# Expert layers with routing woven in: a planner that counts VectorE work by spacing, and ScalarE's copies kept to the first half of a group of matmuls

## The chip, the cores and the metric

The kernel runs on one core of one Trainium2 chip, as one launch. The metric is device time in microseconds (us); three runs of the kernel before gave 767.39, 765.89 and 762.88, so its median is 765.89.

## The reference

Attention with a local window and 32 global tokens gives x, 4352 rows of 512. A gate then gives every row to one of 8 experts of exactly 544 places, greedily by the sorted logits, and each expert applies two layers to its rows:

```python
cap = N // E                              # 4352 // 8 = 544
logits = x @ w_gate
for idx in np.argsort(-logits.flatten()):
    tok, e = (int(idx) // E, int(idx) % E)
    if assigned[tok] >= 0 or counts[e] >= cap:
        continue
    assigned[tok] = e; counts[e] += 1
for e in range(E):
    mask = assigned == e
    out[mask] = np.maximum(x[mask] @ w1[e], 0.0) @ w2[e]
```

w1[e] is 512 x 1024, w2[e] is 1024 x 512, all float32.

## The kernel before, in words

Up to about 230 us of the profile the kernel does the attention (function `attention`), which the change leaves alone. Then a routing phase (`Routing.phase`, L556) finds one expert that fills up next and the 544 rows it gets, and from 277 us on the eight experts run one after another in `ffn` (L873), called groups 0 to 7 here. While TensorE (PE) multiplies for one expert, the routing phase for a later one is woven between its matmuls.

**One group.** First H = relu(x w1): 8 blocks f of 128 hidden columns by 2 halves of the expert's 544 rows; each of these 16 small groups is 12 matmuls of 128x272 (L893), which sum three products of high and low parts (x high by w1 high, x low by w1 high, x high by w1 low). After each, ScalarE (ACT) writes relu of it as `hh`, the high part (L895; for every second one also 32 columns into `h32`, L897), and VectorE (DVE) writes the rest as `hl` (L899, "H's low part"). An H tile lies in one of 4 PSUM buffers, which are free again when `hl` is made. Then small matmuls in plain float32 for the last 32 rows (L908), then four tiles Y = H w2 of 24 matmuls of 128x512 each (L918), each copied out by ACT (L866) and scattered by a DMA of GpSimd's queue (POOL).

**What has to be ready for the next group.** Its weights: `w1r` and `w2r` are gathered by POOL's queue (1 MB each, two of each per expert, L705); ACT copies a slice of 128x512 as the high part (`w1h`, `w2h`, L717), and DVE subtracts for the low part (`w1l`, `w2l`). Of the eight w1 slices, four hold columns that the first four blocks f read, four (tag "b") those of the last four blocks; what of the latter is not made by f = 4 is made there at once (`force(f"b{ph}")`, L885). Its rows: five gathers `xg` by the routing's result `idx`, then 20 transposes on PE into an H tile (L746), `xh` by ACT and `xl` by DVE.

**Routing.** A phase has a search of 8 steps (`search`, L516). A step is 18 small matmuls on PE (`r_G` by `r_oh`, the last of them `rem` by `one`), `r_ce` on DVE, 2 matmuls with `big`, a scan `r_pm` and a compare `r_G` on DVE, and so on: each engine waits for the other. After it come some 30 small DVE instructions, 34 matmuls with `rhs`, and `idx`.

**What sets the order.** Every engine runs its instructions in the order in which the Python program writes them, and waits at an instruction until its input is there. That order comes from a model of time in the program. `V.now` is PE's time: `step(ns)` (L806) adds 125 for an H matmul and 232 for a Y matmul, then writes out whatever has come due: `hl` (list `fill`), the low parts of slices (list `lag`), items of `todo` (gathers, copies, transposes, with a time and a condition each), and the next piece of routing. `V.busy` is DVE's time (`Queue`, L386): each instruction issued through it adds an estimated duration. Routing yields the time at which its next PE piece may be written: `ready()` (L393) is `V.busy` plus HOP. The copies of weight slices wait for `calm()` (L774): DVE less than 200 ns ahead and fewer than two subtractions outstanding. A group's end (L921) waits until everything for the next group has been written.

Of the kernel before, what the change touches and what calls it, by code (L numbers as in the profile page):

```python
# [369 lines left out]
TX = 22000  # L370
TW = 34000
AHEAD = 200
HOP = 400
SLACK = 100
PACE = 250
RELU = 700
# [9 lines left out]
class Queue:  # L386


    def __init__(s, eng):
        s.eng = eng  # L390
        s.now = s.busy = 0.0

    def ready(s):  # L393
        return s.busy + HOP
# [4 lines left out]
    def __getattr__(s, name):  # L399
        op = getattr(s.eng, name)  # L400

        def issue(*args, **kw):
            aps = [x for x in list(args) + list(kw.values()) if hasattr(x, "dtype") and hasattr(x, "shape")]
            n = max(int(np.prod(x.shape[1:])) for x in aps)
            fast = name in ("tensor_scalar", "tensor_copy") or name == "tensor_tensor" and all(
                mybir.dt.size(x.dtype) == 2 for x in aps)
            s.busy = max(s.busy, s.now) + 180 + n * (1.9 if "scan" in name else 0.5 if fast else 1.05)
            return op(*args, **kw)  # L408
        return issue


class Routing:
# [58 lines left out]
    def begin_ps(s, ctx):  # L471
        s.ps = ctx.enter_context(s.tc.tile_pool(name="rps", bufs=1, space=PSUM))

    def mm(s, out, *args, ns=60, **kw):
        s.nc.tensor.matmul(out, *args, **kw)  # L475
        s.V.now += ns
        s.V.busy = max(s.V.busy, s.V.now + 200)

    def t(s, name, shape, dt=F32):
        return s.sb.tile([128] + shape, dt, name="r_" + name)  # L480
# [35 lines left out]
    def search(s):  # L516
        nc = s.nc
        for it in range(NIT):
            yield -1
            yield s.when  # L520
            A = s.ps.tile([128, 2, E], F32, name="R")
            for i in range(18):
                j, r = slice(2 * i, 2 * i + 2), 32 * (i % 4)
                g, o = (s.G[:, j].rearrange("p a b -> p (a b)"), s.oh[:, j]) if i < 17 else (s.one, s.rem)
                s.mm(A[r:r + 32], g, o, ns=22, start=(i < 4), stop=(i >= 14))
            p = s.ps.tile([128, 16, E], F32, name="R2")
            if it == 0:
                lo = s.t("lo", [34], I32)
                lof = s.t("lof", [34])
                s.V.tensor_scalar(lo, s.u, 0xffff, None, op0=ALU.bitwise_and)  # L530
                s.V.tensor_scalar(lof, lo, 2.0 ** -16, None, op0=ALU.mult)
                s.x = s.hi
            else:
                x = s.t("x%d" % (it % 2), [34])
                if it == 3:
                    s.V.scalar_tensor_tensor(x, s.x, P, lof, op0=ALU.subtract, op1=ALU.add)
                else:
                    s.V.tensor_scalar(x, s.x, P, None, op0=ALU.subtract)
                s.x = x
            ce = s.t("ce", [2, 16, E], F16)  # L540
            s.V.tensor_tensor(ce, A[:, :, None, :].to_broadcast([128, 2, 16, E]),
                              s.dk[:, :, :, None].to_broadcast([128, 2, 16, E]), op=ALU.mult)
            when = s.V.ready()
            yield -1
            yield when
            for k in range(2):
                s.mm(p, s.big, ce[:, k], start=(k == 0), stop=(k == 1))
            pm = s.t("pm%d" % (it % 2), [16 * E])
            s.V.tensor_tensor_scan(pm, p.rearrange("p a b -> p (a b)"), s.fin[:, it], 0.0, op0=ALU.max,
                                         op1=ALU.min)  # L550
            P = pm[:, 16 * E - 1:16 * E]
            if it < NIT - 1:
                s.cand(s.x, P, it + 1)
        s.P = P.bitcast(I32)

    def phase(s, ph):  # L556
# [16 lines left out]
        a = s.t("a", [34])  # L573
# [18 lines left out]
        p = s.ps.tile([128, 68], F32, name="R")  # L592
# [4 lines left out]
        if more:  # L597
            g = s.t("gt", [34], BF16)
# [23 lines left out]
        rhs = s.rhs  # L622
# [3 lines left out]
        ohl = s.t("ohl", [64, 34], BF16)  # L626
        for k in range(4):
            q = slice(16 * k, 16 * k + 16)
# [10 lines left out]
        p = s.ps.tile([128, 64], F32, name="R2")  # L639
        for j in range(34):  # L640
            r = 32 * (j % 4)
            s.mm(p[r:r + 32], rhs[:, :, :, j].rearrange("p a b -> p (a b)"), ohl[:, :, j], ns=22, start=(j < 4),
                 stop=(j >= 30))
        if not last:
            s.V.scalar_tensor_tensor(s.act, s.wt, vs, s.act, op0=ALU.not_equal, op1=ALU.mult)
# [13 lines left out]
        p = s.ps.tile([128, 6], F32, name="R2")  # L659
# [26 lines left out]
def experts(ctx, tc, A, xd, ident, rt, out):  # L686
# [55 lines left out]
    def trans_x(xg, t, late):  # L742
        n = sizes[t]
        p = ps.tile([128, 4, 128], F32, name="H", bufs=4)
        for d in range(4):
            nc.tensor.transpose(p[:, d, :n], xg[t][:n, 128 * d:128 * d + 128], ident[:n, :n])  # L746
        q = slice(128 * t, 128 * t + n)
        split(xh[:, :, q], xl[:, :, q], p[:, :, :n], late, SPLIT + 4 * 110)
# [12 lines left out]
    V = rt.V  # L761
    V.now = V.busy = 0.0
    pool, dma, need = [0.0], [0.0], [0.0]
    fill, lag, todo, raw1 = [], [], [], {}
    done, cur, mid, wrote = [False], [0], [-1], [0.0]

    def pool_op(ns, nbytes=0):
# [4 lines left out]
        return pool[0]  # L772

    def calm():  # L774
        return V.busy < V.now + AHEAD and len(lag) < 2

    def chain():
        for ph in range(1, E):
# [10 lines left out]
    def at(tag, t, f, cond=None):  # L789
        todo.append((tag, t, cond, f))  # L790

    def pending(*tags):
        return any(x[0] in tags for x in todo)
# [12 lines left out]
    def step(ns):  # L806
        V.now += ns
        low()
        settle()
        for i, (tag, t, cond, f) in enumerate(todo):  # L810
            if t <= V.now and (cond is None or cond()):
                todo.pop(i)
                f()
                break
        while not done[0] and V.now >= need[0]:
            v = next(routing, None)
            if v is None:
                done[0] = True
            elif v >= 0:
                need[0] = v  # L820
# [21 lines left out]
    def get_x(p):  # L842
        xg = load_x(p)
        for t in range(5):
            r = pool_op(1040, sizes[t] * 2048)
            at(f"x{p}", r, lambda t=t: trans_x(xg, t, True), lambda: mid[0] == p - 1)

    def get_w2(p):
        def go(k):
# [23 lines left out]
    def ffn(ph):  # L873
        nxt = ph + 1
        t0 = V.now
        cur[0] = ph
        half = []
        if nxt < E:
            at(f"g{nxt}", t0, lambda: get_w1(nxt, half), lambda: nxt in rt.widx and not pending(f"b{ph}"))
            at(f"h{nxt}", t0, lambda: get_x(nxt), lambda: nxt in rt.idx and (mid[0] == ph or V.now > t0 + TX))  # L880
            at(f"v{nxt}", t0, lambda: get_w2(nxt), lambda: mid[0] == ph and nxt in rt.widx and
               (not pending(f"h{nxt}") or V.now > t0 + TW))
        for f in range(8):
            if f == 4:
                force(f"b{ph}")  # L885
                half.append(True)
            for hf in range(2):
                q = slice(HF * hf, HF * hf + HF)
                p = ps.tile([128, HF], F32, name="H", bufs=4)
                fs = slice(128 * f, 128 * f + 128)  # L890
                for d in range(4):
                    for k, (w, x) in enumerate(((w1h, xh), (w1h, xl), (w1l, xh))):
                        nc.tensor.matmul(p, w[d][:, fs], x[:, d, q], start=(d + k == 0), stop=(d + k == 5))  # L893
                        step(125)
                nc.scalar.activation(hh[:, f, q], p, AF.Relu)  # L895
                if hf:
                    nc.scalar.activation(h32[:, f], p[:, HF - 32:HF], AF.Relu)  # L897
                low(len(fill) > 1)
                fill.append((V.now + RELU, lambda p=p, f=f, q=q: V.scalar_tensor_tensor(  # L899
                    hl[:, f, q], p, 0.0, hh[:, f, q], op0=ALU.max, op1=ALU.subtract)))  # L900

        low(True)
        force(f"w{ph}")

        p = ps.tile([128, 128], F32, name="Y", bufs=2)
        for f in range(8):
            for c in range(4):
                nc.tensor.matmul(p[32 * c:32 * c + 32], h32[:, f], w2r[f // 4][:, f % 4, 128 * c:128 * c + 128],  # L908
                                 start=(f == 0), stop=(f == 7))
            step(220)  # L910
        mid[0] = ph
        out_tile(ph, 4, p)
        for t in range(4):
            p = ps.tile([128, DM], F32, name="Y", bufs=2)
            for f in range(8):
                q = slice(128 * t, 128 * t + 128)
                for k, (h, w) in enumerate(((hh, w2h), (hh, w2l), (hl, w2h))):
                    nc.tensor.matmul(p, h[:, f, q], w[f], start=(f + k == 0), stop=(f + k == 9))  # L918
                    step(232)
            out_tile(ph, t, p)  # L920
        while nxt < E and (pending(f"g{nxt}", f"h{nxt}", f"a{nxt}", f"x{nxt}", f"v{nxt}") or nxt not in raw1):  # L921
            step(120)
        settle(True)

# [7 lines left out]
    xg = load_x(0)  # L932
# [96 lines left out]
```

## Time and profile before

| | us |
|---|---|
| median of three runs | 765.89 |
| the profiled execution, its own time | 761.97 |
| its span, first to last instruction | 760.2 |
| PE busy | 698.3 |
| DVE busy | 506.1 |
| ACT busy | 305.6 |
| POOL busy | 159.6 |
| groups 0 to 7, from the first H matmul to the last Y matmul | 470.66 |

Names in rows read "written tile <- read tiles"; L12 is line 12 of the kernel. A row of the windows view gives the stretch (us from the span's start), its length, the busy time of PE with the number of instructions, the TensorE clock that was granted (1.00 is full), the share of the DMA engines and GB/s. In a row of the timeline the first two numbers are start and duration, and brackets hold the idle time before and what ended it. A matmul's busy time overlaps the next one's, so the lengths of stretches count, not sums of busy time.

### The profile page before, as it was taken

The page shows a single profiled execution, that of the slowest core. Times are in us where ns is not written, and L with a number is a line of the kernel's source. Part 1 is how long each engine was busy: PE and PEld are TensorE (multiplying, and loading weights), DVE is VectorE, ACT ScalarE, POOL GpSimd, SP SyncE. Part 2 cuts the span into 40 slices and gives each one's busy share as a digit, 9 for nine tenths or more (in the row PEclk, how much of TensorE's full clock was granted, in tenths as well). Part 3 has the DMA queues.
Part 4 walks back from the last instruction along what each step waited for, and adds up shares of the span by engine and source line. Part 5 has one row for each costly group of instructions (what it writes and reads, how often), then busy time and mean ns, then how long its engine had stood idle before and what let it go on. Part 6 is the DMA issues. An engine that isn't in the chain of part 4 may idle for free. (4 is left out here: it accounts for less than half of the span.)

```text
span 760.2 us, 21827 instructions
## 1 busy us (share of the span) xinstructions
PE 698.3 (92%) x9012; PEld 571.8 (75%) x9012; DVE 506.1 (67%) x1855; ACT 305.6 (40%) x841; POOL 159.6 (21%) x190
## 2 busy tenths in 40 slices
PE   7899999999995289989999998999998999999993
PEld 6667777777773179778878877877876987988982
DVE  5787787778686777666776766766766766651400
ACT  4656766656650034233323323414322333552310
POOL 5222221121100130340150043034034015231011
PEclk9999999999997569999999999999999999999998
DMA  8998879869601160260080062054036008251000
GB/s 347 409 364 325 321 276 334 323 239 337 253 20 57 64 217 1 94 233 15 6 304 32 6 252 86 1 176 165 1 106 235 1 12 312 104 199 55 2 32 28
DMA packets 32418, 120.55 MB, mean 159 GB/s; under 512 B 6720, under 2 KB 6976, under 8 KB 24128
## 3 DMA queue, kind: packets, MB, share of 16 engines
q1 hardware_dynamic: 22080, 67.78, 23.9%
q0 software_dynamic: 10240, 51.39, 19.0%
q8 instruction: 71, 1.16, 0.6%
q14 instruction: 27, 0.22, 0.1%
HBM read 101.32 MB, written 17.83 MB: 157 GB/s over the span
## 5 line engine op out<-in xcount | busy, mean ns | idle before, releaser
L893 PE MATMUL H<-xh,w1h 128*128 128x272 f32 x512 | 154.3, 301 | 1.9 <-ACT w1h L717 1.9
L893 PE MATMUL H<-xl,w1h 128*128 128x272 f32 x512 | 153.9, 301 | 2.2 <-DVE xl L408 2.2
L893 PE MATMUL H<-xh,w1l 128*128 128x272 f32 x512 | 151.8, 296 | 1.0 <-DVE w1l L408 1.0
L145 ACT ACTIVATE p<-p,nm 128x128 f32<-128x128 f32 x256 | 81.8, 392 | 67.9 <-DVE ls L165 35.5
L895 ACT ACTIVATE hh<-H 128x272 fp32r<-128x272 f32 x128 | 50.9, 397 | 137.9 <-PE H L893 131.4
L918 PE MATMUL Y<-w2l,hh 128*128 128x512 f32 x256 | 103.2, 403 | 0.0
L918 PE MATMUL Y<-w2h,hh 128*128 128x512 f32 x256 | 103.0, 402 | 0.0
L918 PE MATMUL Y<-w2h,hl 128*128 128x512 f32 x256 | 102.1, 399 | 0.0
L893 PEld LDWEIGHTS H<-xh,w1h 128*128 128x128 f32 x512 | 99.1, 194 | 4.0 <-ACT w1h L717 3.0
L893 PEld LDWEIGHTS H<-xl,w1h 128*128 128x128 f32 x512 | 99.1, 194 | 3.8 <-DVE xl L408 3.2
L893 PEld LDWEIGHTS H<-xh,w1l 128*128 128x128 f32 x512 | 99.0, 193 | 2.2 <-DVE w1l L408 2.1
L408 DVE SCALAR_TENSOR_TENSOR hl<-H,hh 128x272 fp32r<-128x272 f32 x128 | 55.7, 436 | 31.3 <-ACT h L897 20.5
L717 ACT ACTIVATE w1h<-w1r 128x512 fp32r<-128x512 f32 x64 | 37.7, 626 | 94.8 <-DMA w1r<-in_w_dram,widx 58.8
L134 PE MATMUL S<-qk,qz 128*64 128x128 f32 x1024 | 70.5, 279 | 5.7 <-DVE qz L86 3.0
L86 POOL COPY qz<-q 64x544 f32<-64x544 f32 x60 | 38.2, 636 | 149.0 <-DMA q<-in_qk_dram 133.1
L134 PEld LDWEIGHTS S<-qk,qz 128*64 128x64 f32 x1024 | 54.9, 136 | 18.4 <-issue 14.2
L141 DVE CUSTOM_DVE_ANT_0 p<-S,mask 128x128 f32<-128x128 f32 x256 | 58.6, 285 | 6.9 <-DMA mask<-in_mask_dram 2.8
L918 PEld LDWEIGHTS Y<-w2h,hh 128*128 128x128 f32 x256 | 48.1, 188 | 12.7 <-issue 2.8
L918 PEld LDWEIGHTS Y<-w2l,hh 128*128 128x128 f32 x256 | 48.2, 188 | 9.7
L918 PEld LDWEIGHTS Y<-w2h,hl 128*128 128x128 f32 x256 | 48.2, 188 | 9.7
L408 DVE TENSOR_TENSOR w1l<-w1r,w1h 128x512 fp32r<-128x512 f32 x64 | 42.9, 687 | 18.4 <-ACT w1h L717 18.2
L408 DVE TENSOR_TENSOR w2l<-w2r,w2h 128x512 fp32r<-128x512 f32 x64 | 41.9, 685 | 16.2 <-ACT w2h L717 15.4
(165 smaller groups left out, 1130.7 us busy)
## 6 DMA issues: line engine op xcount, KB each, us to landing
vw<-in_vw_dram SPq DMA_DIRECT2D x32, 1040.0 KB, 7.8
qk<-in_qk_dram SPq DMA_DIRECT2D x32, 432.0 KB, 5.4
q<-in_qk_dram SPq DMA_DIRECT2D x32, 272.0 KB, 6.0
xd<-xs SPq DMA_DIRECT2D x8, 1024.0 KB, 6.3
xd<-xg SPq DMA_DIRECT2D x64, 8.0 KB, 5.6
xg<-xd,idx POOLq DMA_INDIRECT x40, 3.7
mask<-in_mask_dram SPq DMA_DIRECT2D x1, 512.0 KB, 6.1
cf<-in_cf_dram SPq DMA_DIRECT2D x1, 512.0 KB, 12.4
```

What stands on the lines that cost most here:

```text
L86: eng.tensor_copy(z[r, :, h, :], q[r].rearrange("p (j i) -> p j i", i=32))
L134: nc.tensor.matmul(st[64 * r:64 * r + 64, c, :], z[:, j].rearrange("p h i -> p (h i)"), kw[:, k0:k0 + 128], start=True, stop=True)
L141: nc.vector.tensor_tensor_reduce(s.p[:, c, :], st[:, c, :], mask[:, 4 * s.u + c, :], 1.0, -BIG, ALU.add, ALU.max, nm[:, c:c + 1])
L145: nc.scalar.activation(s.p[:, c, :], s.p[:, c, :], AF.Exp, bias=nm[:, c:c + 1], scale=SCALE)
L408: return op(*args, **kw)
L717: nc.scalar.activation(hi, raw, AF.Copy)
L893: nc.tensor.matmul(p, w[d][:, fs], x[:, d, q], start=(d + k == 0), stop=(d + k == 5))
L895: nc.scalar.activation(hh[:, f, q], p, AF.Relu)
L918: nc.tensor.matmul(p, h[:, f, q], w[f], start=(f + k == 0), stop=(f + k == 9))
```

## The change

Four numbers or rules of the model of time change; no instruction is added or taken away, only the order in which they are written.

- DVE's estimate of an instruction over n elements per partition: before 180 + 1.05 n (0.5 n for the fast forms, 1.9 n for scans), now 70 + 1.04 n (0.53, 2.05), at least 110, and 90 more when it reads what the last one wrote. HOP falls from 400 to 320. A matmul of routing pushes `V.busy` to 200 ns behind itself before; now by `tail`, 0 for the 18 matmuls of a search step and 100 for the 34 `rhs` matmuls.
- `room`: copies by ACT of weight slices may be written only in the first half of a small group of 12 H matmuls (d < 2), and in the first 21 of 24 Y matmuls (f < 7).
- A transpose of gathered rows is held while three subtractions are outstanding.
- `hl` of every second small group comes due 300 ns later.

```diff
-HOP = 400
+HOP = 320
...
-            s.busy = max(s.busy, s.now) + 180 + n * (1.9 if "scan" in name else 0.5 if fast else 1.05)
+            ns = max(110, 70 + n * (2.05 if "scan" in name else 0.53 if fast else 1.04))
+            if any(x.tensor is s.last for x in aps[1:]):
+                ns += 90
+            s.last = aps[0].tensor
+            s.busy = max(s.busy, s.now) + ns
...
-    def mm(s, out, *args, ns=60, **kw):
+    def mm(s, out, *args, ns=60, tail=200, **kw):
         s.nc.tensor.matmul(out, *args, **kw)
         s.V.now += ns
-        s.V.busy = max(s.V.busy, s.V.now + 200)
+        s.V.busy = max(s.V.busy, s.V.now + tail)
...
-                s.mm(A[r:r + 32], g, o, ns=22, start=(i < 4), stop=(i >= 14))
+                s.mm(A[r:r + 32], g, o, ns=22, tail=0, start=(i < 4), stop=(i >= 14))
...
-            s.mm(p[r:r + 32], rhs[:, :, :, j].rearrange("p a b -> p (a b)"), ohl[:, :, j], ns=22, start=(j < 4),
+            s.mm(p[r:r + 32], rhs[:, :, :, j].rearrange("p a b -> p (a b)"), ohl[:, :, j], ns=36, tail=100, start=(j < 4),
...
-        return V.busy < V.now + AHEAD and len(lag) < 2
+        return room[0] and V.busy < V.now + AHEAD and len(lag) < 2
...
-            at(f"x{p}", r, lambda t=t: trans_x(xg, t, True), lambda: mid[0] == p - 1)
+            at(f"x{p}", r, lambda t=t: trans_x(xg, t, True), lambda: mid[0] == p - 1 and len(lag) < 3)
...
                         nc.tensor.matmul(p, w[d][:, fs], x[:, d, q], start=(d + k == 0), stop=(d + k == 5))
+                        room[0] = d < 2
                         step(125)
...
-                fill.append((V.now + RELU, lambda p=p, f=f, q=q: V.scalar_tensor_tensor(
+                fill.append((V.now + RELU + 300 * hf, lambda p=p, f=f, q=q: V.scalar_tensor_tensor(
...
                     nc.tensor.matmul(p, h[:, f, q], w[f], start=(f + k == 0), stop=(f + k == 9))
+                    room[0] = f < 7
                     step(232)
```

The order in which the changed program writes its instructions is known from building it. In group 2, the end of the routing for the next expert moves on PE, and with it what hangs on it. These are PE's rows at the end of group 2 before: Y matmuls (`hh` or `hl` by a slice of w2), the transposes of `xg` into H tiles, and the next search step (`r_oh`, `r_G`).

```order
L918 MATMUL Y<-w2l_4843,hh 128x512
L746 MATMUL H<-ident,xg 128x128 x4
L918 MATMUL Y<-w2h_4835,hl 128x512
L918 MATMUL Y<-w2h_4836,hh 128x512
L918 MATMUL Y<-w2l_4844,hh 128x512
L746 MATMUL H<-ident,xg 128x128 x4
L918 MATMUL Y<-w2h_4836,hl 128x512
L746 MATMUL H<-ident,xg 128x128 x8
L475 LDWEIGHTS r_G
```

And these are the same transposes now, of the same group on PE; they stand among the first 10 of its 96 Y matmuls.

```order
L925 MATMUL Y<-w2h_4829,hl 128x512
L751 MATMUL H<-ident,xg 128x128 x4
L925 MATMUL Y<-w2h_4830,hh 128x512
L751 MATMUL H<-ident,xg 128x128 x4
L925 MATMUL Y<-w2l_4838,hh 128x512
L751 MATMUL H<-ident,xg 128x128 x4
L925 MATMUL Y<-w2h_4830,hl 128x512
L480 LDWEIGHTS big
```

Before, 16 of the 20 transposes stand within the last four Y matmuls of the group and 4 behind them and behind a search step; now the next search steps and 86 Y matmuls follow all 20. The same holds in every group from 1 to 5; in group 0 they stand behind the 58th to 68th Y matmul.

On ACT, these are the rows around f = 4 of group 2 before: `hh` and `h` are the copies of H, `w1h` the high parts of the same group's second four blocks, `w2h` those of its second layer.

```order
L897 ACTIVATE h_4851<-H 128x32
L717 ACTIVATE w2h_4830<-w2r_4845 128x512
L895 ACTIVATE hh<-H 128x272 x2
L897 ACTIVATE h_4851<-H 128x32
L717 ACTIVATE w1h_4823<-w1r 128x512
L717 ACTIVATE w1h_4824<-w1r 128x512
L895 ACTIVATE hh<-H 128x272 x2
```

The two `w1h` rows are the ones that `force` writes at f = 4. Now all four of these second-half copies stand on ACT a group earlier, between the copies of group 1's Y tiles:

```order
L872 ACTIVATE y<-Y 128x512
L722 ACTIVATE w1h_4821<-w1r 128x512
L722 ACTIVATE w1h_4822<-w1r 128x512
L872 ACTIVATE y<-Y 128x512
L722 ACTIVATE w1h_4823<-w1r 128x512
L722 ACTIVATE w1h_4824<-w1r 128x512
L872 ACTIVATE y<-Y 128x512 x2
L722 ACTIVATE w2h_4829<-w2r_4845 128x512
```

So in groups 1 to 5 nothing is left for `force` to write. On POOL's queue, last, these are the gathers of group 2 before, in whose middle the routing for the next expert ends: its w1 and w2 (`w1r`, `w2r`) by halves, rows of group 2's output (`out_dram`), and at the end the next expert's rows (`xg`).

```order
L705 DMA w1r<-in_w_dram,widx 128x2048
L705 DMA w2r_4845<-in_w_dram,widx 128x2048
L758 DMA out_dram<-y,idx 4352x512
L705 DMA w1r<-in_w_dram,widx 128x2048
L705 DMA w2r_4846<-in_w_dram,widx 128x2048
L758 DMA out_dram<-y,idx 4352x512
L705 DMA xg<-xd,idx 128x512 x4
L705 DMA xg<-xd,idx 32x512
```

And now, on the same queue, for the same expert; the first row is the output of the group before:

```order
L763 DMA out_dram<-y,idx 4352x512 x4
L710 DMA w1r<-in_w_dram,widx 128x2048 x2
L710 DMA xg<-xd,idx 128x512 x4
L710 DMA xg<-xd,idx 32x512
L710 DMA w2r_4845<-in_w_dram,widx 128x2048
L760 DMA out_dram<-yr,idx_6715 17408x128
L710 DMA w2r_4846<-in_w_dram,widx 128x2048
L763 DMA out_dram<-y,idx 4352x512 x3
```

The rows `xg` now stand ahead of the group's own output and of the next w2, behind two loads of w1.

More of the change, by code (lines that the diff above doesn't have):

```diff
@@ L391, in __init__ @@
         s.now = s.busy = 0.0
+        s.last = None
     def ready(s):
@@ L764, in experts @@
     fill, lag, todo, raw1 = [], [], [], {}
+    room = [True]
     done, cur, mid, wrote = [False], [0], [-1], [0.0]
@@ L921, in ffn @@
         while nxt < E and (pending(f"g{nxt}", f"h{nxt}", f"a{nxt}", f"x{nxt}", f"v{nxt}") or nxt not in raw1):
+            room[0] = True
             step(120)
```

## The prediction

> **What bounds the kernel now.** I read the page first, then the lengths of the eight groups, then pieces of them, then PE's waits. The page says which engine is full, and where its clock fell:
>
> ```profile
> PE 698.3 (92%) x9012; PEld 571.8 (75%) x9012; DVE 506.1 (67%) x1855; ACT 305.6 (40%) x841; POOL 159.6 (21%) x190
> PEclk9999999999997569999999999999999999999998
> ```
>
> PE is at 92%, and no other engine is near. The order of the attention and of the first routing phase doesn't change, so only the groups matter. In the windows view, one row per group, 0 first:
>
> ```profile
> 277.39:339.69 62.30, 60.09 (x591) 0.96 0.35 128
> 339.69:400.92 61.23, 59.64 (x573) 0.97 0.29 106
> 400.92:463.63 62.71, 59.95 (x574) 0.97 0.30 104
> 463.63:523.89 60.26, 58.47 (x574) 1.00 0.31 108
> 523.89:585.06 61.17, 58.58 (x573) 1.00 0.31 106
> 585.06:646.52 61.46, 59.54 (x557) 0.97 0.31 106
> 646.52:699.50 52.98, 52.65 (x410) 1.00 0.34 122
> 699.50:748.05 48.55, 48.55 (x353) 1.00 0.07 24
> ```
>
> Group 7, with no routing and nothing to prepare, takes 48.55 us and PE never rests. Group 6, whose next rows are transposed early in its Y part, takes 52.98. Groups 0 to 5 take 60.3 to 62.7, with 8 search steps each. What a search step costs PE shows in the 49th to 96th H matmul of group 2 (38 routing matmuls among them) and of group 7 (none):
>
> ```profile
> 409.90:416.96 7.06, 7.06 (x88) 1.00 0.00 0
> 705.51:711.52 6.01, 6.01 (x50) 1.00 0.00 0
> ```
>
> 1.05 us for 38 matmuls, 0.55 for a step of 20: 8 steps are 4.4 us, far from the 8 to 10 by which groups 0 to 5 exceed group 6. So the rest is waiting. PE's own waits, from 277 us on:
>
> ```profile
> PE H L746 <- DMA xg<-xd,idx: 6.5, 8, 1.0
> PE H L893 <- DVE xl L408: 2.2, 5, 0.5
> PE H L893 <- ACT w1h L717: 1.9, 5, 0.4
> PE H L746 <- DVE xl L408: 1.1, 1, 1.1
> PE H L893 <- DVE w1l L408: 1.0, 5, 0.2
> ```
>
> They fall in two places: at a group's end, where transposes wait for gathered rows and the first H matmuls for `xl`, and at f = 4 (five times `w1h`, five times `w1l`). No search matmul waits for DVE anywhere. The waits' sum, 12.7 us, is less than what they cost, because a matmul's end is modelled and the clock falls behind some of them; so I measure both places as stretches.
>
> **The change, first place: the group's end.** From the last Y matmul to the 49th H matmul of the next group, for boundaries 0/1 to 5/6, with their sum, and then the same stretch 6/7:
>
> ```profile
> 335.14:348.14 13.00, 10.79 (x104) 0.87 0.20 68
> 397.58:409.90 12.32, 10.80 (x104) 0.86 0.21 71
> 459.79:471.26 11.47, 9.45 (x104) 1.00 0.27 94
> 520.98:531.51 10.53, 9.33 (x104) 1.00 0.23 81
> 581.36:594.11 12.75, 10.92 (x104) 0.87 0.24 80
> 644.90:654.79 9.89, 9.56 (x99) 1.00 0.16 58
> sum 69.96, PE 60.85; mean PE 10.14
> ...
> 699.26:705.51 6.25, 6.25 (x50) 1.00 0.12 45
> ```
>
> Without a wait these 49 matmuls take 6.25 us. The other work in the six stretches stays somewhere on PE: 12 transposes each, and 40 routing matmuls in the first five and 36 in the sixth, 236 at 1.05/38 = 0.028 us, 6.5 us. A transpose's price comes from the Y parts of group 6 (20 of them inside) and group 7 (none):
>
> ```profile
> 674.82:699.26 24.44, 24.44 (x119) 1.00 0.32 121
> 725.53:747.65 22.12, 22.12 (x99) 1.00 0.10 39
> ```
>
> 2.32/20 = 0.116 us, so 72 cost 8.4 us. Lost at the six boundaries: 69.96 - 6 x 6.25 - 6.5 - 8.4 = 17.6 us. In three of them the granted clock is 0.87, 0.86 and 0.87: 13.00 x 0.13 + 12.32 x 0.14 + 12.75 x 0.13 = 5.1 us of the 17.6 are clock, the other 12.5 are waits and what they bring with them. The order shows why this goes: in groups 1 to 5 all 20 transposes now stand behind the 2nd to 22nd Y matmul, with 74 or more Y matmuls (0.23 us each, 22.12/96) between them and the next H. What is late next there is the gather itself. The issue of one on POOL, and the median time from issue to landing:
>
> ```profile
> L705 POOL DMA_INDIRECT xg<-xd,idx x35 | 37.7, 1077 | 15.2 <-issue 8.2 <-DVE idx L408 6.0 <-PE H L893 0.6
> ...
> xg<-xd,idx POOLq DMA_INDIRECT x40, 3.7
> ```
>
> The first is there after 3.7 us, the fifth after 3.7 + 4 x 1.08 = 8.0. The program writes them 23 Y matmuls ahead of the first transpose in group 0 (5.3 us), in groups 2 to 5 after the 150th to 177th H matmul (0.125 us each, 6.01/48, so 1.9 to 5.3 us, and then the last 32 rows' matmuls and 2 to 4 Y), and only in group 1 at the H part's very end, with 9 Y matmuls to the first transpose and 22 to the fifth: 2.1 and 5.1 us plus the last 32 rows' and some routing matmuls. So group 1 may wait some tenths up to the 1.0 us of the waits above; I count it below. The `xg` now pass the group's output and the w2 loads on POOL's queue; the w2 loads go behind them, and are first read at the next group's start, about 20 us later.
>
> **Second place: f = 4.** The 97th to 108th H matmul, in groups 1 to 5 (group 5 and the sum of the five), and in group 0, where nothing is forced, with the same two routing matmuls:
>
> ```profile
> 601.17:604.03 2.86, 2.27 (x17) 1.00 0.00 0
> sum 14.26, PE 11.36; mean PE 2.27
> ...
> 293.67:295.36 1.69, 1.69 (x16) 1.00 0.00 0
> ```
>
> 14.26 - 5 x 1.69 = 5.8 us. The order has these copies a group earlier, so all of it goes; nothing else is due at that point.
>
> **What the change adds: shorter notice between DVE and PE.** Search pieces are now written closer together, with PE's whole queue behind each. How much slack there was: the shortest hand-overs with PE loaded are in group 2, those without any pacing in the first phase, where PE has nothing else.
>
> ```profile
> 408.27 0.42 DVE L408 TENSOR_TENSOR r_ce<-R,dk 128x256 f16<-128x256 f32 x1 [0.65 <-PE R L475]
> 409.48 0.28 PE L475 MATMUL R<-r_ce,big 128*128 128x128 f16 x2
> ...
> 243.57 0.79 DVE L408 SCALAR_TENSOR_TENSOR r_G<-r_x,r_pm,cf 128x544 f16<-128x544 f32 x1
> 244.27 0.24 DVE L408 TENSOR_SCALAR r_x<-r_x,r_pm 128x34 f32<-128x34 f32 x1
> 244.78 0.42 DVE L408 TENSOR_TENSOR r_ce<-R,dk 128x256 f16<-128x256 f32 x1 [0.28 <-PE R L475]
> 245.26 0.37 PE L475 MATMUL R<-r_ce,big 128*128 128x128 f16 x2 [0.55 <-DVE r_ce L408]
> ```
>
> Loaded, 0.79 us pass from the end of `r_ce` to its matmul; unpaced 0.06. Slack 0.73. The diff takes from the planner's notice 0.20 (tail), 0.08 (HOP) and 0.11 (180 + 1.05 x 256 against 70 + 1.04 x 256): 0.34 us are left. So no search step waits by itself. `r_G` also shows that the new estimate fits: the next instruction starts 0.70 us behind it although it lasts 0.79, and 70 + 1.04 x 544 + 90 is 726 ns. [...]
>
> What can eat the 0.34 is an instruction in front that waits for ACT, which the planner doesn't count:
>
> ```profile
> DVE hl L408 <- ACT h L897: 20.5, 30, 1.1
> DVE hl L408 <- ACT hh L895: 10.7, 15, 1.0
> ```
>
> 45 waits of 0.69 us on average. The `+300` takes 0.3 from the first kind, leaving 0.38, about the slack; the 15 others exceed it by 0.37. If each of those delays a search piece, that is 15 x 0.37 = 5.6 us; if all had enough behind them, 0. I take half, 3 us, with group 1's gathers in it. Below nothing it can't go, since no search matmul waits now. The other edits (`room`, three outstanding subtractions, 36 ns for `rhs`) cost nothing while ACT is at 40% and x's low parts have a whole Y part's cover; without that cover they would be the waits for `xl` above, again at a boundary.
>
> **Sum.** -17.6 - 5.8 + 3 = -20.4 us against the profiled execution: its own time was 761.97 (span 760.2 and 1.8 around it), so 741.6; I say 741. The runs' median, 765.89, lies 3.9 above this execution, which may be more boundaries at the lower clock (1.7 each); with none left the medians should come together.
>
> **Rivals.**
>
> *The clock stays low.* The waits go, but PE's clock still falls at some boundaries, since transposes, routing and Y mix there. Then the 5.1 us stay, or come at other places: 746. For it: two boundaries with waits kept 1.00, so waits alone don't decide. Against: stretch 6/7, without waits, also kept 1.00. [...] Chance 0.15.
>
> *Slower: PE waits for DVE at the hand-overs.* 48 search steps have two each, 96. DVE runs its queue in order, so if it is late by more than its slack at each, PE stands still with the H matmuls behind it. From 23.4/96 = 0.24 us each it turns the gain into a loss. If half of them wait as long as `hl` does for ACT, 0.69 us, that is +33 - 23.4: 772. For it: DVE at 67% does more in less time. Against: the slack of 0.34, and estimates that fit the rows. Chance 0.06.
>
> *No change: rows still arrive at the end.* Two w1 loads now stand right before the `xg` in POOL's queue; if they hold them up, the boundaries keep their 17.6 and only f = 4 is won: 761.97 - 5.8 + 3 = 759. Against: outside group 1 they have 4 us and more from writing to use, by the counts above, and the w1 loads are written 100 and more H matmuls earlier in groups 2 to 5. Chance 0.07.
>
> **How the numbers follow.** Forecast 0.72, by itself 734 (no new wait, and waits within the Y parts gone too) to 749 (new waits of 10 us). The range 732 to 755 holds it and the clock's rival and leaves out 0.13. 0.5% is 3.8 us here, about what a measurement can tell: faster 0.72 + 0.15 = 0.87, same 0.07, slower 0.06.
>
> **What would show it.** Right: groups 1 to 5 near 57 us; stretches from the last Y to the 49th H near 8 or less with the clock at 1.00; 1.5 to 1.7 us at f = 4; no PE wait for `xg` or for `w1l`. New rows of PE waiting for `r_G` or `r_ce` price the added term: 3 us expected, over 23 would make it slower. Boundaries still at 0.87 would be the clock's rival, PE waits for `xg` the last one.

## The result, and the profile after

| | before | after |
|---|---|---|
| median of five runs, us | 765.15 (762.88 to 767.39) | 738.46 (737.97 to 740.89) |
| the profiled execution, its own time | 761.97 | 740.89 |
| its span | 760.2 | 739.1 |
| groups 0 to 7, first H to last Y matmul | 470.66 | 447.70 |

The ratio is 0.9658 (95% interval 0.9631 to 0.9686), so the change makes the kernel 3.4% faster; 741 was forecast. The profiled execution after is the longest of its five. In it the first H matmul comes at 279.47 us, 2.1 us later than in the one before, although the order up to there is the same; so the groups are the thing to compare: 23.0 us less.

The page after, its line of busy times:

```profile
PE 688.0 (93%) x9012; PEld 565.3 (76%) x9012; DVE 501.7 (68%) x1855; ACT 307.0 (42%) x841; POOL 161.8 (22%) x190
```

The engines do the same number of instructions; what went is time between them, and on PE also 10.3 us of busy time, which stalls and the lower clock had stretched: before, an H matmul is busy for 0.43 us at half clock (at 341.00) and for 0.39 right behind a wait (at 602.47), against 0.29 undisturbed (at 601.17). The windows view shows where, one row per group, here 0 to 5 and the sum of all eight:

```profile
279.47:341.01 61.54, 61.54 (x632) 0.96 0.35 131
341.01:400.65 59.64, 59.64 (x652) 1.00 0.31 109
400.65:459.40 58.75, 58.19 (x594) 1.00 0.35 118
459.40:518.80 59.40, 59.22 (x628) 1.00 0.32 114
518.80:577.16 58.36, 58.36 (x592) 1.00 0.30 107
577.16:627.86 50.70, 50.70 (x373) 1.00 0.36 128
...
sum 447.70, PE 446.95; mean PE 55.87
```

From group 1 on the clock is 1.00, and PE is busy almost throughout. Routing now runs ahead: it ends within group 4, so group 5 has none, and groups 0 and 1 hold more of it (632 and 652 PE instructions, 591 and 573 before). From the last Y matmul to the 49th H matmul of the next group, boundaries 0/1, 2/3, 5/6 and the sum of the six:

```profile
340.78:348.24 7.46, 7.46 (x91) 1.00 0.11 38
...
459.17:467.02 7.85, 7.85 (x88) 1.00 0.72 274
...
627.63:633.89 6.26, 6.26 (x50) 1.00 0.66 246
sum 42.33, PE 42.33; mean PE 7.05
```

The second is the longest: all lie under 8, at full clock, and the last, with no routing in it, takes the 6.25 of the undisturbed stretch 6/7. The 97th to 108th H matmul, group 1, group 5 and the sum of 1 to 5:

```profile
355.45:357.36 1.91, 1.91 (x32) 1.00 0.00 0
...
589.18:590.69 1.51, 1.51 (x15) 1.00 0.00 0
sum 8.35, PE 8.35; mean PE 1.67
```

And PE's waits from 277 us on, all of them (`issue` is idle time for which the profile shows nothing that PE waited for):

```profile
PE H L751 <- DMA xg<-xd,idx: 0.8, 1, 0.8
PE H L751 <- issue: 0.6, 1, 0.6
PE R L480 <- DVE r_ce L413: 0.2, 1, 0.2
```

12.7 us of PE waits have become 1.6, and only 0.7 of these lie in the groups: the wait for `xg` is at 278.0 us, ahead of the first H matmul, for group 0's own rows. One hand-over of a search step shows as a wait, by 0.2 us.

### The profile page after: what moved, and what is told of

The parts are those of the page before. It is cut to its first block, busy times and chain, and to the rows that moved or that the text cites. A ratio compares the mean times of both kernels' runs of the same rounds, so it can differ in the third digit from the quotient of the medians.

```text
span 739.1 us, 21853 instructions
## 1 busy us (share of the span) xinstructions
PE 688.0 (93%) x9012; PEld 565.3 (76%) x9012; DVE 501.7 (68%) x1855; ACT 307.0 (42%) x841; POOL 161.8 (22%) x190
## 3 DMA queue, kind: packets, MB, share of 16 engines
q8 instruction: 71, 1.16, 0.6%
## 4 chain that ended last, share of the span: by engine, by line
PE 60%; DMA 1%; issue 1%; POOLq 0%; DVE 0%; ACT 0%; ACTq 0%
PE H L899 27%; PE Y L925 25%; PE R L480 4%; PE H L751 2%; PE Y L915 2%; DMA xg<-xd,idx 1%; DMA out_dram<-y,idx 0%; POOLq L1034 0%; ACT y L872 0%; DVE hl L413 0%; DVE r_ce L413 0%; ACT h L904 0%; DVE r_x L413 0%; ACTq L872 0%; ACT hh L902 0%
## 5 line engine op out<-in xcount | busy, mean ns | idle before, releaser
L899 PE MATMUL H<-xl,w1h 128*128 128x272 f32 x512 | 150.4, 294 | 0.0
L899 PE MATMUL H<-xh,w1h 128*128 128x272 f32 x512 | 150.2, 293 | 0.0
L899 PEld LDWEIGHTS H<-xh,w1h 128*128 128x128 f32 x512 | 97.5, 190 | 0.7 <-issue 0.2
L899 PEld LDWEIGHTS H<-xl,w1h 128*128 128x128 f32 x512 | 97.4, 190 | 0.7 <-issue 0.2
L899 PEld LDWEIGHTS H<-xh,w1l 128*128 128x128 f32 x512 | 97.3, 190 | 0.6 <-issue 0.2
L413 DVE SCALAR_TENSOR_TENSOR hl<-H,hh 128x272 fp32r<-128x272 f32 x128 | 55.0, 434 | 31.2 <-ACT h L904 22.2
L872 ACT ACTIVATE y<-Y 128x512 f32<-128x512 f32 x32 | 19.2, 599 | 135.1 <-PE Y L925 112.4
L763 POOL DMA_INDIRECT out_dram<-y,idx x32 | 31.7, 991 | 155.3 <-ACT y L872 143.7
```

The source lines that it names most:

```text
L763: nc.gpsimd.indirect_dma_start(out=out, out_offset=bass.IndirectOffsetOnAxis(ap=rt.idx[ph][:n, t:t + 1], axis=0), in_=y[:n], in_offset=None)
L872: nc.scalar.activation(y[:n], p[:n], AF.Copy)
```

## The experiments

My theory was the prediction's: shorter notice for the search lets routing end earlier in a group, so that the next rows are there before the Y part and the next w1 copies before f = 4; the three rules (`room`, at most two subtractions outstanding, `+300`) carry nothing. Against it stood: the rules carry it; the two places are only where the time shows and not what costs it; the notice of the hand-overs has a price. Ratios are to the kernel before, run on the same chip.

**1. The model alone**: the changed kernel without its three rules.

```diff
-        return room[0] and V.busy < V.now + AHEAD and len(lag) < 2
+        return V.busy < V.now + AHEAD and len(lag) < 2
-            ..., lambda: mid[0] == p - 1 and len(lag) < 3)
+            ..., lambda: mid[0] == p - 1)
-                fill.append((V.now + RELU + 300 * hf, ...
+                fill.append((V.now + RELU, ...
```

> The change without room, without the limit of three outstanding subtractions and without the 300 ns: only the estimates of DVE's work, HOP and tail. Theory: the estimates let the routing run ahead, and that alone brings rows and second-half weights early, so nearly all of the gain stays: 737 to 743 us. Rival: the gain needs ACT's copies kept out of the second half of a small group, since hl waits for ACT and search pieces wait behind hl; then PE waits for r_G and r_ce and the time is 746 to 755.

Measured: 737.28 (736.93 to 738.31), ratio 0.9658 (0.9607 to 0.9709), the ratio of the whole change. The rules carry nothing that can be measured.

**2. The rules alone**: the same three lines put into the kernel before (with the lines that set `room`), its model of time unchanged.

> The kernel before with room, the limit of three and the 300 ns, but the old estimates of DVE's work. Theory: the routing still ends late in each group, rows and two second-half slices of w1 are still late, and room even leaves fewer moments for copies: 762 to 772 us, no gain. Rival (the rules on ACT's copies carry the gain): 745 to 752.

Measured: 763.52 (760.23 to 767.26), ratio 1.001 (0.9978 to 1.0041). No gain; at f = 4 the stretches still took 2.55 to 2.87 us in groups 1 to 6. Runs 1 and 2 together put the whole change on the model of time.

**3. Rows early, transposes late**: the changed kernel, but transposes may be written only in the last three Y matmuls of a group, though their rows have landed long before. This puts back one of the boundaries' two costs, the late `xl`, without the late gathers.

```diff
-            ..., lambda: mid[0] == p - 1 and len(lag) < 3)
+            ..., lambda: late[0] and mid[0] == p - 1 and len(lag) < 3)
...
                     room[0] = f < 7
+                    late[0] = t == 3 and f == 7
```

> The change with the 20 transposes of each next expert held until the last Y matmuls, though their rows have been gathered long before, at all seven boundaries. Theory: most of the 17.6 us at the boundaries was waiting for rows that came late and the clock behind it, so with rows there only the chain transpose, xh, xl before the first H matmul is exposed, about 0.75 us each: 742 to 746 us. Rival: transposing right before the next group is what costs, by that chain and by the clock, whatever the rows do: 751 to 758.

Measured: 746.91 (745.03 to 749.96), ratio 0.9796 (0.9737 to 0.9855): 8.4 us more than the change, a little over my 742 to 746 and under the rival's 751 to 758. Boundaries 0/1 and 6/7 in its windows:

```profile
337.19:349.74 12.55, 10.62 (x105) 0.86 0.06 23
...
681.13:689.45 8.32, 8.07 (x64) 1.00 0.09 33
```

and two of its PE waits:

```profile
PE H L900 <- DVE xl L413: 2.1, 7, 0.7
PE H L751 <- issue: 1.5, 1, 1.5
```

Boundary 6/7 is clean, and 4/5 and 5/6 take the same 8.32: 8.32 - 6.25 - 12 x 0.116 = 0.68 us that PE stands still until `xl` is made. My expectation had about this for all seven. But with 0.028 us taken off for each routing matmul, boundaries 1/2 to 3/4 (9.83, 8.97 and 10.24 us) lose 1.3 to 1.6 each, two of them with a transpose that waits 0.6 us for an earlier one, and 0/1 loses 3.8: 12.55 x 0.14 = 1.8 of clock and the one wait of 1.5 us for issue are in it. The seven lose 10.2 us; six of the change's seven lost 1.0 and the last nothing. The difference of 9.2 is nearer to the 9.6 by which this run lies above run 1, which ran on the same chip, than to the 8.4 against the change, measured on another. So of the 2.9 us that each boundary lost before (17.6/6), 0.7 to 1.6 was the late transposes by themselves; the rest was rows that came late, and the clock.

**4. Two copies held back to f = 4**: the changed kernel, but of the four second-half copies of w1 only two may be made ahead.

```diff
-                   lambda: mid[0] == p - 1 and not pending(...) and calm())
+                   lambda k=k: k == 0 and mid[0] == p - 1 and not pending(...) and calm())
```

> The change with two of the four second-half copies of w1 of each expert held until f = 4, in groups 1 to 7. Theory: that costs what it cost before, 5.8 us in five groups, so 1.16 in each of seven, 8.1 us: 745 to 748 us, with 2.8 us for the 97th to 108th H matmul. Rival (with DVE and ACT less crowded at that point, the copies are over before PE needs them): 738 to 741.

Measured: 746.67 (746.47 to 748.15), ratio 0.9781 (0.973 to 0.9833): 8.2 us over the change, 8.1 expected, and 9.4 over run 1 on the same chip. One of its seven stretches at f = 4, that of group 7, without any routing, and the sum of the seven:

```profile
696.54:699.41 2.87, 2.27 (x15) 1.00 0.00 0
sum 20.60, PE 16.39; mean PE 2.34
```

The waits there are short, and do not add up to that price:

```profile
PE H L899 <- DVE w1l L413: 2.4, 7, 1.1
PE H L899 <- ACT w1h L722: 1.8, 5, 0.4
```

4.2 us of waits, 8.2 to 9.4 us of time. The same seven stretches take 11.37 us in the change, 9.2 less: measuring a place by its stretch, and not by the waits shown in it, gave the right price here.

**5. The new estimates without the shorter notice**: the changed kernel, rules included, with HOP at 400, 200 ns behind every routing matmul and 22 ns for `rhs`, as before.

> The change with HOP back at 400 and the tails back at 200 (and 22 ns per rhs matmul): the new estimates of DVE's instructions and the three rules stay. The order has the transposes behind the 2nd to 39th Y matmul in groups 1 to 5 and behind the 64th to 72nd in group 0, and nothing forced at f = 4. Theory: where they stand in the Y part doesn't matter as long as rows are there and no group's end is left open, so all of the gain stays: 736 to 742 us. Rival: every earlier step counts, and half of the gain goes: 746 to 755.

Measured: 740.80 (739.75 to 741.99), ratio 0.9688 (0.9644 to 0.9732). The estimates of DVE's instructions alone bring nearly all of the gain (the rules bring none, by runs 1 and 2).

**6. The shorter notice without the new estimates**: the kernel before with HOP 320, the two `tail` values and 36 ns for `rhs`.

> The kernel before with HOP 320 and the new tails alone. The order has the gathers 12 to 13 Y matmuls earlier and the transposes behind the 77th to 96th Y matmul; two copies are still forced at f = 4 in groups 2 to 5. Theory: four forced places at 1.16 us, 4.6 us, stay lost, and of the boundaries' 17.6 only about 0.5 us each: 744 to 750 us. Rival (what counts is to be far ahead, not just in time): 753 to 762.

Measured: 758.41 (755.75 to 763.28), ratio 0.9927 (0.9884 to 0.9969). My 744 to 750 was wrong, and the rival's number right, but not for the reason that it gave: the boundaries 1/2 to 4/5 were as good as the change's, at 7.0 us each. The loss had gone to f = 4. The boundary 1/2, and f = 4 in groups 2 and 3:

```profile
399.25:406.28 7.03, 7.03 (x73) 1.00 0.21 77
413.42:417.58 4.16, 2.34 (x15) 1.00 0.01 4
474.72:478.88 4.16, 2.34 (x15) 1.00 0.00 0
```

4.2 us where before it was 2.9, and 4.4 and 4.2 in groups 4 and 5. The timeline of group 2 there shows why, DVE's and ACT's rows with the H matmul that waits:

```profile
413.89 1.15 ACT L717 ACTIVATE w1h<-w1r 128x512 fp32r<-128x512 f32 x2
...
414.11 0.79 DVE L408 SCALAR_TENSOR_TENSOR r_G<-r_x,r_pm,cf 128x544 f16<-128x544 f32 x1
...
414.81 1.28 DVE L408 TENSOR_TENSOR w2l<-w2r,w2h 128x512 fp32r<-128x512 f32 x2
416.01 1.28 DVE L408 TENSOR_TENSOR w1l<-w1r,w1h 128x512 fp32r<-128x512 f32 x2
...
416.75 0.39 PE L893 MATMUL H<-xh,w1l 128*128 128x272 f32 x1 [1.66 <-DVE w1l L408]
```

ACT has both `w1h` by 415.04 (413.89 + 1.15), but on DVE `r_G` and two low parts of w2, written earlier, stand ahead of the forced `w1l`, which starts at 416.01. The copies fell due together with a search step, and in three groups of four such a stall was followed by at least 3.41 us at half clock (the rows are in the last section).

**7. No notice beyond the estimates**: the changed kernel with HOP = 0.

> The change with HOP 0 in place of 320: every search piece is written 0.32 us earlier. In the trace of the change the shortest time from the end of r_ce to its matmul is 0.20 us and of r_G 0.29, typical ones 0.41 and 0.35, against 0.05 unpaced, so about 0.30 to 0.36 us of slack are typical. Theory: PE begins to wait for DVE at the shorter ones, 0.1 us at about half of 96 hand-overs, and gathers that come sooner in groups 0 and 1 give back up to 2: 737 to 744 us, with rows of PE waiting for r_ce and r_G. Rival (DVE cannot go faster, every piece waits its 0.32): 755 to 770.

Measured: 741.76 (741.12 to 743.39), ratio 0.9699 (0.9654 to 0.9744). From the end of `r_ce` to its matmul now pass 0.05 us in the median of the 48 hand-overs, as in the first phase (here 345.44 + 0.42 to 345.91):

```profile
345.44 0.42 DVE L413 TENSOR_TENSOR r_ce<-R,dk 128x256 f16<-128x256 f32 x1
345.91 0.27 PE L480 MATMUL R<-r_ce,big 128*128 128x128 f16 x2
```

And yet the profile lists no wait of PE from 277 us on. PE does wait, by less than is listed: at 0.05 us it is already there when `r_ce` is done. Its starts in the trace show by how much. Beyond the usual distance from the matmul before (0.125 us behind an H matmul, 0.23 behind a Y matmul, 0.06 behind others) the 96 hand-overs take 8.3 us here, 6.0 in the change and 6.7 in the kernel before; and the eight groups take 450.4 us, 2.7 more than in the change. The ratio can't be told from the change's, so between medians this cost is not shown; but to take away the last 0.3 us of notice wins nothing, and seems to cost some 2 us.

**8. Written too early**: the changed kernel with HOP = -400, to see whether the slower rival's mechanism exists.

> The change with HOP -400: search pieces are written 0.72 us earlier than in the change, which is 0.36 to 0.42 us too early at typical slack. It prices the rival of the prediction, PE waiting for DVE at hand-overs. Theory: each of 96 hand-overs stops PE for about 0.4 us, 38 us, and three more groups force copies at f = 4: 770 to 790 us, slower than before. Rival: PE catches up at the next hand-over, since DVE gains the time that PE loses, and the waits come to less than half: 745 to 760.

Measured: 772.78 (771.73 to 774.11), ratio 1.0103 (1.0056 to 1.0149): slower than before, as expected. Group 0:

```profile
277.12:354.73 77.61, 69.19 (x772) 0.98 0.29 107
```

and the two greatest of PE's waits:

```profile
PE R L480 <- DVE r_G L413: 11.0, 31, 0.4
PE R L480 <- DVE r_ce L413: 3.3, 10, 0.9
```

41 of 96 hand-overs show a wait, 14.3 us together, and all routing is done by group 3. It costs 34 us against the change. Counted by PE's starts as in run 7, the hand-overs take 33.7 us where the change's take 6.0: 27.7 us more, 0.29 us for each of the 96. Of the rest, some 3.5 us are three stalls at f = 4, in groups 0, 1 and 2 (3.41, 2.82 and 2.87 us). So between a notice of 0 and one of -0.4 us the hand-overs turn from nearly free to dearer than all that the early rows bring.

**9. Run 6 with its forced copies one block earlier**: as run 6, but what is missing for f = 4 is written at f = 3.

```diff
-            if f == 4:
+            if f == 3:
                 force(f"b{ph}")
+            if f == 4:
                 half.append(True)
```

> The kernel before with HOP 320 and the new tails, as in the sixth experiment, and the copies that were forced at f = 4 written at f = 3, 24 H matmuls (3 us) before PE needs them; the gathers and transposes stay within a few Y matmuls of where they were. In the sixth experiment the 97th to 108th H matmul took 4.16 to 4.40 us in groups 2 to 5 and four half-clock stretches came with it. Theory (its missing gain lies at f = 4): 10 us of waits and up to 7 of clock come back: 741 to 749 us. Rival (rows that come just in time cost more than the boundary stretches show): 752 to 759.

Measured: 741.41 (739.57 to 745.52), ratio 0.971 (0.9669 to 0.9751): 17.0 us less than run 6 by moving one line (16.6 by the two ratios, since the chips differ). The stretch at f = 4 in group 4, the longest, and the sum of 1 to 5:

```profile
523.30:525.60 2.30, 2.11 (x35) 1.00 0.00 0
...
sum 9.34, PE 9.10; mean PE 1.82
```

The one in group 4 holds some 20 routing matmuls more than that of group 1, which takes 1.51 us. The half-clock stretches are gone, and the boundaries take 7.0 to 8.0. So the stall at f = 4 was what run 6 lacked, with the clock that fell behind it; and routing need not run a group ahead as in the change: rows by the Y part and copies before f = 4 are enough.

**10. A shorter notice without the rules**: run 1 with HOP = 240, in search of something faster.

> The new estimates without the three rules (as in the first experiment) and with HOP 240 in place of 320. The gathers of groups 0 and 1 are written earlier against their use, and slack of about 0.2 us is left at typical hand-overs. Theory: waits for gathered rows are all that is still to be had, up to 2 us, and PE hardly waits for DVE: 735 to 738 us. Rival (shorter notice costs more than the rows give): 739 to 743.

Measured: 739.30 (738.17 to 743.73), ratio 0.9679 (0.9647 to 0.971). Not the 735 to 738 that I hoped for but inside the rival's 739 to 743, and no difference from run 1 or the change that could be measured. No version beat the change.

## Why the prediction was right, point by point

**Boundaries, 17.6 us.** 42.33 less 6 x 6.25 leaves 4.8. The six stretches show 91, 72, 88, 99, 50 and 50 instructions, but some of them began ahead of the stretch, among them some 10 of the 99; 139 routing matmuls start inside, worth 139 x 0.028 = 3.8 us. So 1.0 us is still lost, and 16.6 are won. The clock's part was right: no boundary is below 1.00. Run 3 shows how the waits' part divides: 0.7 us for each boundary is the chain to `xl` by itself, and up to 1.6 where routing stands between.

**f = 4, 5.8 us.** 14.26 - 8.35 = 5.9. Run 4 puts the cost back and finds 8.2 us for seven places (8.2/7 = 1.17 each; 5.8/5 = 1.16 forecast), or 9.4 against run 1 on its own chip; that the first agrees so closely is in part luck.

**New waits, 3 us.** As waits, the groups show 0.7 us: 0.2 at a hand-over and 0.6 at a transpose. Measured by length, with 0.116 us taken off for each transpose and 0.028 for each routing matmul, the H parts outside the two places became 1.9 us longer (131.3 to 133.2). So the term came to something between 0.7 and 2.7 us (1.9 with these two waits), less than the 3 that I took. The one hand-over that waits has the `hl` in front that I had in mind, held up by ACT; but it waits for `h`, the kind that I had put at about the slack, not for `hh`, the 15 that I had priced:

```profile
488.80 0.44 DVE L413 SCALAR_TENSOR_TENSOR hl<-H,hh 128x272 fp32r<-128x272 f32 x1 [0.47 <-ACT h L904]
...
489.30 0.42 DVE L413 TENSOR_TENSOR r_ce<-R,dk 128x256 f16<-128x256 f32 x1
...
489.77 0.27 PE L480 MATMUL R<-r_ce,big 128*128 128x128 f16 x2 [0.18 <-DVE r_ce L413]
```

It happens once in 96, where I had taken half of 15. DVE's waits for ACT did not shrink: from 270 us on,

```profile
DVE hl L413 <- ACT h L904: 22.2, 23, 1.1
...
DVE hl L413 <- ACT hh L902: 8.6, 12, 1.0
```

30.8 us against 31.2, fewer and longer; run 1, without the rules, has 17.4 and 14.0. So `+300` did not relieve the waits for `h`, as I had it do, and but for this one they do not reach PE either. The slack for that is there: `r_ce`'s hand-overs take 0.41 us in the median, 0.36 more than the 0.05 of an unpaced one (forecast 0.34). But the shortest, next to the one that waits, takes 0.20. And the prediction read `r_ce`'s 0.79 us as the shortest hand-over before; `r_G`'s were shorter, down to 0.58, and are 0.29 at the least and 0.35 in the median now. They had enough left too, but that was not worked out.

**Sum.** In the groups 16.6 + 5.9, less the 1.9 by which the H parts grew, give 20.6, and 23.0 were measured. The rest lies in the Y parts, which became 2.5 us shorter by the same counting (183.5 to 181.0, with the new wait of 0.6 in it): 20.6 + 2.5 = 23.1. One piece is a wait of 0.9 us for `xg` inside group 5's Y part before; the others are not traced to a cause. The forecast named such waits for its lower end and did not count them. The profiled execution's 740.89 against 741.6 forecast is partly luck: the 2.1 us later start covers most of what the sum was short of. Between medians the gain is 26.7 us, 3.7 more than between the groups: the median before lies 3.2 us above its profiled execution, and the one after 2.4 below its own. Where the clock fell only profiled executions show. But the record has the mean granted clock of 33 more executions of the kernel before: the 11 fastest take 760.9 us on average at 0.9603, the 11 slowest 766.4 at 0.9554. 0.0049 x 764 is 3.7 us of the 5.5 between them, estimated so, which supports the clock as the larger part of the spread.

**Gathers.** I had group 1 at risk; it waited for nothing. The 0.8 us for `xg` lie ahead of group 0, and the 0.6 for "issue" is at a transpose in group 2's Y part.

**Group lengths.** "Near 57" for groups 1 to 5 holds for their mean (286.85/5 = 57.4), not for the rows: 58.4 to 59.6 in four with routing, 50.7 in one without. Before, groups 0 to 5 exceeded group 6 by 7.3 to 9.7 us, not by 8 to 10; nothing hangs on it.

**Rivals.** The clock that stays low fell: all rows from the first boundary on show 1.00. (Before, three boundaries with waits had kept 1.00, not two.) Rows that still arrive at the end: fell, 1.0 us left at six boundaries. PE waiting at the hand-overs: exists (run 8), at a notice 0.72 us shorter than the change's.

## What to carry to other kernels

A planner that writes for in-order engines (in run 6 `w1l` starts on DVE at 416.01, behind the two `w2l`, though its `w1h` is there at 415.04) should count an instruction by the spacing to its successor, measured in the trace (0.70 us for `r_G` there, 414.11 to 414.81, though it lasts 0.79). What that wins is not busy time but an earlier due time for all that hangs on the planned work; so look for the places where something is made at the last moment (here transposes at the boundary and copies at f = 4), measure them as stretches between fixed instructions, and move what is late there one place earlier, as run 9's one line did. A shorter notice was nearly free down to HOP 0 (run 7: 8.3 us at all hand-overs, 6.0 in the change), and at HOP -400 each hand-over paid 0.29 us (run 8).

## What the runs showed of the hardware that was not expected

**The half clock came in windows on a grid.** In the profile before, the three half-clock stretches at boundaries each last 3.41 us (3.413 in the trace's record of the clock), and the other two start 61.44 and 245.76 us after the first, which is 18.0 and 72.0 times 3.413. The windows of that grid at the boundaries 0/1, 1/2, 2/3 and 4/5, and those at half clock behind them:

```profile
336.57:339.98 3.41, 1.49 (x28) 1.00 0.34 120
339.98:343.39 3.41, 3.41 (x18) 0.50 0.20 77
398.01:401.42 3.41, 2.26 (x32) 1.00 0.54 173
401.42:404.83 3.41, 3.04 (x13) 0.50 0.20 77
459.45:462.86 3.41, 1.86 (x13) 1.00 0.52 162
...
582.33:585.74 3.41, 2.23 (x31) 1.00 0.45 157
585.74:589.15 3.41, 3.25 (x15) 0.50 0.22 82
```

Run 6 shows such a grid too (538.27 and 603.12 lie 35.0 and 54.0 windows behind 418.80):

```profile
415.39:418.80 3.41, 2.05 (x29) 1.00 0.02 5
418.80:422.21 3.41, 3.41 (x17) 0.50 0.00 0
476.83:480.24 3.41, 2.19 (x30) 1.00 0.00 0
...
534.85:538.27 3.42, 1.84 (x14) 1.00 0.00 0
538.27:541.68 3.41, 3.17 (x29) 0.50 0.02 5
599.71:603.12 3.41, 1.75 (x16) 1.00 0.00 0
603.12:606.53 3.41, 3.41 (x33) 0.50 0.00 0
```

The windows ahead of the drops have PE busy for 1.49, 2.26 and 2.23 of 3.41 us before, and for 2.05, 1.84 and 1.75 in run 6; no single wait is longer than 1.7. Two with as little (1.86 and 2.19) were followed by full clock, so over all of them modelled busy time alone does not decide. The windows before hold 8 to 12 transposes each; in run 6, where there are none, busy time does sort them: the three up to 2.05 were followed by half clock, the one at 2.19 was not. What sets off the half clock is not shown. Where in the grid a stall falls may matter for its price: of the two stretches of the same 4.16 us at f = 4 in run 6, the one in group 2 was followed by a window at half clock (418.80) and the one in group 3 by none. The first begins 1.45 us behind the start of a window, the second 1.31, and the second's next window is busy for just these 0.14 us more. One pair does not show it, though.

**Waits showed less than they cost.** Run 4's 4.2 us of waits cost 8.2 to 9.4 us, with the clock at 1.00 in the row shown: 2.87 us of which 2.27 are busy, for twelve matmuls that take 1.51 where nothing stalls them.
